# Gate values applied at the eviction of the expert rows instead of on the gathered rows

## The chip, the cores and the metric

One core of a Trainium2 chip runs one program. The metric is device time in microseconds (us) of one execution. The engines are named as in the profile: PE (matmuls; PEld is its weight load), ACT or ScalarE, DVE or VectorE, POOL or GpSimd (here mostly gathers, which are indirect DMAs), and SP, whose queue issues most DMAs.

## The reference, cut to what matters

The program is a block-sparse softmax attention (4 batches, 8 heads, 576 rows), then an expert layer with sticky routing, then a second, dense expert attention. The change is in the middle layer and at its seam with the last:

```python
logits = einsum('bsd,de->bse', x, w_gate)          # 8 experts
local_gate = sigmoid(x @ w_local)
for b: prev_e = -1
    for s:
        fresh_e = argmax(logits[b, s])
        e = fresh_e if s == 0 or local_gate[b, s] < 0.5 or prev_e < 0 else prev_e
        prev_e = e
        p = exp(logits[b, s] - max); p /= p.sum() + 1e-9
        h = maximum(x[b, s] @ w1[e], 0)             # 512 -> 1024
        out[b, s] = p[e] * (h @ w2[e])              # 1024 -> 512
x = out                                             # input of the last layer
```

`p[e]`, one number for each of the 2304 rows, is the gate value that the change moves.

## The kernel before

Stage 1 (`stage1`) computes attention for 16 pairs of heads. Its order is written out by hand: each step has a time in units of its own (W, EARLY, S0, TX0), and each engine runs its instructions in the order of these times, then in the order in which the later code emits them. S0 says when the copies of the first expert's weights (`split0`) are emitted: `split_high` makes a high part (f32r) on ScalarE and gives back a function that makes the low part on VectorE. At 146.70 stage 1 emits `rows_ev`, which copies the last rows out (`xraw`), and at 149.21 the copy `XT` on which the last logits rest.

`Route.main` then sorts the rows by expert. It is a chain of small steps, mostly on VectorE with small matmuls between (`small`). So that PE has work, `fill(i)` emits FILL[i] pieces of the first expert tile between them (`start`: 16 pieces of the first layer, six matmuls of 256 columns each, in four accumulators, and 16 of the second, three matmuls of 512 columns each). Their evictions (`hT_ev`) wait in `M.late` until they are popped or flushed. `inv` lists, for each slot of an expert tile, the row that it takes; `slot` lists for each row its slot. At the end of `main`, VectorE computes `psel`, the gate value of each row, in the layout of the rows (128 x 20), and `M.hoist` splits the last two of the first expert's w2 pieces (5 and 7).

`moe` runs the expert tiles of SEQ: pairs of 128 rows ("P") or tiles of 288 or 352 rows ("L"), t = 0 to 8. For each, the rows are fetched by POOL from `x_dram` through `inv` (`fetch`, four `xg` buffers, some two tiles ahead), turned (`tx`), put through the first layer (`g1`, accumulators `acc`) and the second (`g2`, banks `py`), and evicted by ScalarE (`y_ev`) to a tile that SP stores to `yg` in DRAM by slot. Before tile 1, LEFT says how many of the 32 pieces are left when each of its three transpositions is emitted; `M.tell` then writes the list of experts, from which SP reads the number of the expert for each weight load, and six `load()` of 1 MB each are emitted on SP. After the routing, a further pool `mop2` gives two more `acc` banks and one more `py` bank; `bank("py")` takes the two `py` banks of the first pool and then that one, in turn.

`stage3` fetches the rows of the expert layer from `yg` through `slot` (`fetch3`), and `xscale` multiplies them by `psel` (on VectorE for batch 0, on POOL for the others) before `txx` turns them.

Of the kernel before, what the change touches and what calls it, by code (L numbers as in the profile page):

```python
# [9 lines left out]
F32 = mybir.dt.float32  # L10
# [21 lines left out]
NCOL = 34  # L32
# [479 lines left out]
class Route:  # L512
# [224 lines left out]
    def main(self, fill, first):  # L737
# [47 lines left out]
        self.M.late.pop(0)()  # L785
        n = R[:, S - 1:S]
# [63 lines left out]
        first()  # L850
        slot = C.tile([128, 20], I32, name="slot")
# [41 lines left out]
        v.tensor_copy(erow[:, NT:], fl)  # L893
        den = W.tile([128, 20], F32, name="den")
        psel = C.tile([128, 20], F32, name="psel")
# [10 lines left out]
        self.slot, self.erow, self.psel = slot, erow, psel  # L906

        self.tell = lambda: v.tensor_copy(erow[:, 0:NT], er)
# [78 lines left out]
def moe_ops(nc, K, R, E, M, yg, W, bank, seq, reg):  # L987
# [108 lines left out]
    def y_ev(t, u, keep=False):  # L1096
        s = chunks(t)[u]
        c, m = cols(*seq[t])[u], s.stop - s.start
        y = R.row() if keep else E.tile([128, DM], F32, name="y", tag="xTP" + "hl"[ny[0] % 2])
        ny[0] += 1  # L1100
        if s.stop == width(t) and packed(t):
            lo = W.tile([128, DM], F32, name="ylo", tag="xg", bufs=4)
            nc.scalar.activation(lo[0:m], ys[t][u][m:2 * m], AF.Copy)
            nc.vector.tensor_tensor(y[0:m], ys[t][u][0:m], lo[0:m], op=ALU.add)
        else:
            nc.scalar.activation(y[0:m], ys[t][u][0:m], AF.Copy)
        if keep:
            late[c] = y[0:m]
        else:
            nc.sync.dma_start(yg[128 * c:128 * c + m], y[0:m])  # L1110
# [8 lines left out]
def moe(tc, nc, K, R, E, M, yg, W, ctx):  # L1119
# [24 lines left out]

    def gather():
        if rows:
            M.fetch(rows.pop(0))
# [27 lines left out]
    def start():  # L1175
        hT[0] = []
        for i in range(4):
            p = P1.tile([128, 512], F32, name="acc", bufs=2)
            for k in range(4):
                for f in range(2):  # L1180
                    h_mm(0, p[:, 256 * f:256 * f + 256], 2 * i + f, k, k == 0 and f == 0)
                if k == 3:
                    M.late.append(lambda p=p, i=i: hT_ev(0, p, i, 0))
                yield
        ys[0] = [bank("py") for _ in range(2)]
        for i in range(4):
            for u in range(2):
                for f in range(2):
                    y_mm(0, i, u, f)
                    if i == 3 and f == 1:  # L1190
                        M.late.append(lambda u=u: y_ev(0, u))
                    yield

    def hoist():
        for c in (5, 7):
            *wc[0, c], rest = split_high(nc, E, R.piece(0, c), 0, c)
            rest()
# [10 lines left out]
    P2.append(ctx.enter_context(tc.tile_pool(name="mop2", bufs=1, space=PSUM)))  # L1208
    M.last()
    ws, erow, fetch, fetch3, xscale = M.ws, M.erow, M.fetch, M.fetch3, M.xscale  # L1210
# [8 lines left out]
    for _ in range(6):  # L1219
        load()  # L1220
    for _ in pieces:
        M.flush()
# [35 lines left out]
    for j in range(4):  # L1258
        lab(xscale, 0, j)
# [6 lines left out]
def more(tc, nc, K, R, M, yg, ctx):  # L1266
# [12 lines left out]
    def again(kind, n, end):  # L1279
# [3 lines left out]
        with tc.If(nc.values_load(M.erow[0:1, f:f + 1], min_val=0, max_val=1) > 0):  # L1283
            seq.append((kind, n))
            t = len(seq) - 1
            for i, c in enumerate(cols(kind, n)):
                M.fetch(c, W)
                o.tx(t, i)
# [46 lines left out]
def stage3(tc, nc, K, ws, xr, fetch, xscale, row, out, last=None, nb=B):  # L1335
# [365 lines left out]
    for b in range(nb):  # L1701
        G = 2 * NJ * b
        for j in range(5):
# [38 lines left out]
FILL = (3, 1, 4, 2, 1, 1, 3, 2, 1, 1)  # L1742
# [5 lines left out]
S0 = ((138.5, 140), (140.3, 142), (144.7, 145.3), (144.95, 145.35), (146.68, None), (146.71, 146.9))  # L1748
LEFT = (13, 9, 4)
# [9 lines left out]
def model(tc, cst, qT, qx, kT, vp, tau, wgl, w12, wqk, wv, wo, out):  # L1759
    nc = tc.nc  # L1760
    with ExitStack() as ctx:
        C = ctx.enter_context(tc.tile_pool(name="c", bufs=1))
        DR = ctx.enter_context(tc.tile_pool(name="dr", bufs=1, space=DRAM))
        x_dram = DR.tile([B, S, DM], F32, name="x_dram")
        yg = DR.tile([NCOL * 128, DM], F32, name="yg")
        K = Consts(tc, nc, C, cst)
        L = C.tile([128, 5, B, 9], F32, name="L")
        with ExitStack() as mx, ExitStack() as rx:
# [3 lines left out]
            rt = Route(tc, nc, K, L, C, X, E)  # L1772
            M = Box()
            M.xg, M.split0, M.low, M.routed = {}, {}, {}, False
# [45 lines left out]
            M.late = []  # L1820
# [28 lines left out]
            def xscale(b, j):  # L1849
                x = xr[b, j]  # L1850
                eng = nc.gpsimd if b else nc.vector
                eng.tensor_scalar(x, x, rt.psel[:, 4 * j + b:4 * j + b + 1], 1.0, op0=ALU.mult, op1=ALU.mult)

            def last():
                rx.close()
                M.erow, M.tell = rt.erow, rt.tell
                M.ws = Weights3(tc, nc, ctx, wqk=wqk, wv=wv, wo=wo)

            M.fetch, M.fetch3, M.xscale, M.last = fetch, fetch3, xscale, last
            next(work)  # L1860
            rt.main(fill, first)
            M.routed = True
# [3 lines left out]
        done = stage3(tc, nc, K, ws, xr, fetch3, xscale, R.row, out)  # L1866

        f = 2 * (PMAX + LMAX)
        with tc.If(nc.values_load(M.erow[0:1, f:f + 1], min_val=0, max_val=1) > 0, preferred_fallthrough_block=True):
            with ExitStack() as rest, tc.manual_schedule():  # L1870
                more(tc, nc, K, R, M, yg, rest)
            for j in range(4):
                fetch3(0, j, j)
                xscale(0, j)
            stage3(tc, nc, K, ws, xr, fetch3, xscale, R.row, out, done)
# [64 lines left out]
```

## Time and profile before

| | us |
|---|---|
| median of 3 timed runs (744.45 to 745.25) | 745.1 |
| the profiled execution | 746.25 |
| its span, first to last instruction | 744.5 |
| PE busy | 721.5 (97%) |
| VectorE busy | 545.3 (73%) |
| ScalarE busy | 490.3 (66%) |
| POOL busy | 285.9 (38%) |

The page says how long each engine was busy, the chain of waits leads back from the last instruction, and the timeline shows each instruction with the idle time of its engine before it and, behind an arrow, what ended it. Stage 1 ends at about 285 us, routing and the first tile at about 316, the expert tiles at about 536. PE's clock was granted at full speed (0.998) throughout.

### The profile page before, as it was taken

To read this page: it belongs to the slowest core of one execution; us is meant where nothing else is said; L and a number is where in the kernel's file an instruction comes from. 1 tells how busy PE (TensorE), PEld (TensorE's weight loads), DVE (VectorE), ACT (ScalarE), POOL (GpSimd) and SP (SyncE) were. 2 spreads that over 40 slices of the span, in tenths; PEclk is the share of its full clock that TensorE was granted. 3 is DMA by queue.
4 is the path that set the end of the run, shared out by engine and by line. 5 is a ranking of instruction groups with operands and counts; after the bars stand their busy time and mean duration, and the time that the engine had idled before them with its cause. 6 is when DMAs were issued, how large, how long until landed. Compare 5 with 4: busy or idle time off the path is not lost.

```text
span 744.5 us, 14233 instructions
## 1 busy us (share of the span) xinstructions
PE 721.5 (97%) x5063; PEld 611.2 (82%) x5063; DVE 545.3 (73%) x1427; ACT 490.3 (66%) x1026; POOL 285.9 (38%) x442
## 2 busy tenths in 40 slices
PE   5999999999999999999999999999999999999996
PEld 4788887888887778798889889989788888888874
DVE  7998999899988988625575475554359888878780
ACT  5888888788887785334554455544256787777783
POOL 5888888887777892400110110000366000000000
PEclk9999999999999999999999999999999999999999
DMA  8448534444342431495855756601333000100103
GB/s 282 141 125 304 159 117 147 122 162 131 116 133 66 157 136 31 106 364 171 279 201 184 255 193 212 215 1 53 96 86 99 2 16 1 44 15 30 44 31 101
DMA packets 37408, 95.40 MB, mean 128 GB/s; under 512 B 4336, under 2 KB 14832, under 8 KB 33232
## 3 DMA queue, kind: packets, MB, share of 16 engines
q1 hardware_dynamic: 30960, 73.62, 29.1%
q0 software_dynamic: 5360, 19.34, 8.5%
q10 hardware_dynamic: 1008, 1.44, 0.6%
q8 instruction: 42, 0.69, 0.4%
q14 instruction: 38, 0.31, 0.1%
HBM read 75.58 MB, written 18.81 MB: 127 GB/s over the span
## 4 chain that ended last, share of the span: by engine, by line
PE 87%; DVE 7%; ACT 4%; issue 1%; DMA 1%; ACTq 0%; SPq 0%; DVEq 0%
PE py L1082 16%; PE acc L1053 15%; PE Y L336 11%; PE S L246 9%; PE X L293 8%; PE AV L1646 4%; PE X L1595 3%; PE Y L371 2%; PE S L251 2%; PE misc L1408 1%; PE misc L1409 1%; PE misc L1445 1%; PE S L1525 1%; PE misc L1410 1%; PE misc L1447 1%; PE misc L1446 1%
## 5 line engine op out<-in xcount | busy, mean ns | idle before, releaser
L280 DVE SCALAR_TENSOR_TENSOR P<-S,nm,E 128x576 f32<-128x576 f32 x144 | 116.4, 815 | 10.2 <-ACT E L267 4.6
L257 DVE TENSOR_REDUCE nm<-S 128x1 f32<-128x576 f32 x144 | 105.9, 754 | 17.6 <-PE S L246 16.8
L1082 PE MATMUL py<-w2h,hT 128*128 128x512 f32 (+2 forms) x344 | 114.8, 400 | 0.0
L267 ACT ACTIVATE E<-S,nm 128x576 f32<-128x576 f32 x144 | 104.1, 747 | 6.9 <-DVE nm L257 6.4
L246 PE MATMUL S<-KK,QS 128*128 128x288 f32 x256 | 84.2, 344 | 7.5 <-DVE QS L219 5.6
L293 PE MATMUL X<-cst,P 128*128 128x128 f32 x576 | 87.1, 278 | 1.4 <-ACT PT L304 0.7
L1777 POOL DMA_INDIRECT xg<-x_dram,inv x22 | 24.0, 1089 | 159.8 <-PE px L1011 128.2
L293 PEld LDWEIGHTS X<-cst,P 128*128 128x128 f32 x576 | 67.0, 142 | 16.1 <-issue 7.5
L304 ACT ACTIVATE PT<-X 128x512 f32<-128x512 f32 x128 | 75.7, 605 | 3.9 <-PE X L293 1.1
L1053 PE MATMUL acc<-xTh,w1h 128*128 128x256 f32 (+2 forms) x256 | 76.4, 299 | 0.0
L1053 PE MATMUL acc<-xTl,w1h 128*128 128x256 f32 (+2 forms) x256 | 76.0, 297 | 0.0
L1053 PE MATMUL acc<-xTh,w1l 128*128 128x256 f32 (+2 forms) x256 | 75.9, 297 | 0.0
L1082 PEld LDWEIGHTS py<-w2h,hT 128*128 128x128 f32 (+2 forms) x344 | 63.0, 183 | 15.4
L246 PE MATMUL S<-KL,QS 128*128 128x288 f32 x256 | 73.3, 300 | 0.3 <-DVE KL L201 0.3
L1082 PE MATMUL py<-w2l,hT 128*128 128x512 f32 (+2 forms) x176 | 69.5, 395 | 0.1
L336 PE MATMUL Y<-PT,v 128*64 128x320 f32 (+1 forms) x512 | 69.1, 412 | 0.2 <-ACT G L604 0.2
L1045 DVE SCALAR_TENSOR_TENSOR hT<-acc,hT 128x352 fp32r<-128x352 f32 (+3 forms) x60 | 30.4, 519 | 45.0 <-ACT hT L1042 45.0
L1042 ACT ACTIVATE hT<-acc 128x352 fp32r<-128x352 f32 (+2 forms) x52 | 26.2, 507 | 55.8 <-PE acc L1053 49.6
L246 PEld LDWEIGHTS S<-KK,QS 128*128 128x128 f32 x256 | 49.8, 194 | 9.0 <-issue 7.7
L336 PEld LDWEIGHTS Y<-PT,v 128*64 128x64 f32 x512 | 33.8, 136 | 24.5 <-issue 4.8
L1846 POOL DMA_INDIRECT raw<-yg,slot x18 | 17.6, 977 | 86.9 <-DMA yg<-y 62.0
L246 PEld LDWEIGHTS S<-KL,QS 128*128 128x128 f32 x256 | 50.0, 195 | 0.6 <-DVE KL L201 0.6
(397 smaller groups left out, 1920.6 us busy)
## 6 DMA issues: line engine op xcount, KB each, us to landing
raw<-in_w_dram SPq DMA_DIRECT2D x32, 1024.0 KB, 6.3
kraw<-in_kT_dram SPq DMA_DIRECT2D x15, 608.0 KB, 4.5
QS<-in_qT_dram POOLq DMA_DIRECT2D x15, 576.0 KB, 6.0
v<-in_vp_dram SPq DMA_DIRECT2D x16, 320.0 KB, 3.0
yg<-y SPq DMA_DIRECT2D x17, 256.0 KB, 5.0
qraw<-in_qx_dram SPq DMA_DIRECT2D x15, 288.0 KB, 2.7
x_dram<-xr SPq DMA_DIRECT2D x16, 256.0 KB, 2.5
yg<-raw SPq DMA_DIRECT2D x1, 3072.0 KB, 12.9
```

The lines of the kernel that those rows point to most:

```text
L246: nc.tensor.matmul(o, QS[p % NQ][:, a, cs], k[i][:, sl(576 * a)], start=(n == 0), stop=(n == 1))
L257: nc.vector.tensor_reduce(nm[:, 0:1], t[:, :, :288], axis=AX.XY, op=ALU.min)
L267: nc.scalar.activation(e, t[:, :, :288], AF.Exp, scale=-1.0, bias=nm[:, 0:1])
L280: nc.vector.scalar_tensor_tensor(PP[p, c][:, S * a:S * a + S].rearrange("p (h n) -> p h n", h=2), t[:, :, :288], nm[:, 1:2], e, op0=ALU.is ...
L293: nc.tensor.transpose(x[:, 128 * kc:128 * kc + 128], pp[:, o:o + 128], ident)
L304: nc.scalar.activation(PT[p, h][:, a, :, f:f + 128], x.rearrange("p (k q) -> p k q", k=4), AF.Copy)
L336: nc.tensor.matmul(out, l, r, start=s, stop=e, skip_group_check=True)
L1042: nc.scalar.activation(h[..., 0:w], p, AF.Relu)
L1045: nc.vector.scalar_tensor_tensor(h[..., low(t, c)], p[..., c], 0.0, h[..., c].bitcast(F32), op0=ALU.max, op1=ALU.subtract)
L1053: nc.tensor.matmul(o, a[:, fs], x[:, k, 0:w], start=(first and n == 0), stop=(k == 3 and n == 2), skip_group_check=True)
L1082: nc.tensor.matmul(ys[t][u][0:m], hT[t][i][:, f, k], w[:, 512 * f:512 * f + 512], start=(i == 0 and f == 0 and n == 0), stop=(i == 3 and f ...
L1646: nc.tensor.matmul(o[half(a), f:NH[h]], l, r, start=(k == 0), stop=(k == (1, 4)[h]), skip_group_check=True)
```

## The change

- `psel` is no longer computed at the end of `Route.main` but in a new function `scales`, called as `M.finish()` after `M.tell()` and the six `load()`. It now also turns `psel` on PE (a 128 x 20 transposition in the bank `prest`), copies the result on ScalarE (`pselT`) and stores it by row to DRAM with five DMAs on SP (4 partitions by up to 128 values each).
- `weigh(c)` is new: POOL gathers the gate values of the slots of column c from that DRAM tensor through `inv` into one column of `M.scale` (128 elements of 4 bytes). Nine columns (tiles 0 to 3) are gathered right after `M.finish()`, the 13 others each behind the fetch of its rows.
- `y_ev` multiplies by the column as it evicts (`scale=` of the activation; a second VectorE operation for the packed tail of tile 1). `xscale` is gone from stage 3.
- The evictions of tile 0 (`y_ev(0, u)`) no longer follow its last pieces but come after `g1(1, 2)`.
- The high parts of w2 pieces 5 and 7 are emitted earlier in `main` (after the scan `R`), their low parts after `first()` and where `hoist` stood. The copy of w2 piece 4 in stage 1 moves from 146.68 to 146.705, behind `rows_ev`.
- The first of the four accumulators of `start` takes a `py` bank. FILL and LEFT change; 22 pieces instead of 19 are emitted within `main`, and 27 instead of 28 before the third transposition. The pool `mop2` is opened after `M.finish()`.

```diff
@@ Route.main
         self.M.late.pop(0)()
+        self.M.hoist()
@@
         first()
+        self.M.lows[0]()
         slot = C.tile([128, 20], I32, name="slot")
@@
         nc.scalar.activation(ex, ex, AF.Exp)
-        self.M.hoist()
+        self.M.lows[1]()
         fill(8)
         self.flush()
+        self.slot, self.erow = slot, erow
+        self.tell = lambda: v.tensor_copy(erow[:, 0:NT], er)
+        self.finish = lambda: self.scales(ctx, W, ex, po, fl, pe, NT, px)
+
+    def scales(self, ctx, W, ex, po, fl, pe, NT, px):
+
+        nc, v = self.nc, self.nc.vector
         v.tensor_tensor(fl[:, NT:], fl[:, PMIN:PMIN + 1], fl[:, PMAX + LMIN:PMAX + LMIN + 1], op=ALU.max)
...
         v.tensor_tensor(psel, psel, den, op=ALU.mult)
-        for i in range(2):
-            v.tensor_copy(psel[64:128, 16 + 2 * i:17 + 2 * i], psel[0:64, 17 + 2 * i:18 + 2 * i])
+        pt = px[0:20, 128:256]
+        nc.tensor.transpose(pt, psel, self.K["ident"])
+        sT = W.tile([20, 128], F32, name="pselT")
+        nc.scalar.activation(sT, pt, AF.Copy)
+        for j in range(5):
+            w = min(128, S - 128 * j)
+            nc.sync.dma_start(self.psel[:, 128 * j:128 * j + w], sT[B * j:B * j + B, 0:w])
         ctx.close()
@@ y_ev
+        sc = M.scale[0:m, c:c + 1]
...
-            nc.vector.tensor_tensor(y[0:m], ys[t][u][0:m], lo[0:m], op=ALU.add)
+            nc.vector.tensor_tensor(lo[0:m], ys[t][u][0:m], lo[0:m], op=ALU.add)
+            nc.vector.tensor_scalar(y[0:m], lo[0:m], sc, None, op0=ALU.mult)
         else:
-            nc.scalar.activation(y[0:m], ys[t][u][0:m], AF.Copy)
+            nc.scalar.activation(y[0:m], ys[t][u][0:m], AF.Copy, scale=sc)
@@ moe
+    scaled = [c for t in range(4) for c in cols(*seq[t])]
+
     def gather():
         if rows:
-            M.fetch(rows.pop(0))
+            c = rows.pop(0)
+            M.fetch(c)
+            if c not in scaled:
+                M.weigh(c)
@@ start
-            p = P1.tile([128, 512], F32, name="acc", bufs=2)
+            p = P1.tile([128, 512], F32, name="acc", bufs=2) if i else PY.tile([128, 512], F32, name="py", bufs=2)
@@ moe
     M.tell()
     for _ in range(6):
         load()
+    M.finish()
+    for c in scaled:
+        M.weigh(c)
+    P2.append(ctx.enter_context(tc.tile_pool(name="mop2", bufs=1, space=PSUM)))
+    M.last()
     for _ in pieces:
         M.flush()
@@
             lab(g1, t, i)
             if t > 1:
                 splits(t, 4 + i)
+            elif i == 2:
+                for u in range(2):
+                    lab(y_ev, 0, u)
@@
-    for j in range(4):
-        lab(xscale, 0, j)
@@ stage3
                 at(G - 20 + j, 9, fetch, b, j)
-                at(G - 18 + j, 8, xscale, b, j)
@@
-FILL = (3, 1, 4, 2, 1, 1, 3, 2, 1, 1)
+FILL = (3, 1, 5, 2, 1, 1, 3, 2, 0, 4)
-S0 = ((138.5, 140), (140.3, 142), (144.7, 145.3), (144.95, 145.35), (146.68, None), (146.71, 146.9))
-LEFT = (13, 9, 4)
+S0 = ((138.5, 140), (140.3, 142), (144.7, 145.3), (144.95, 145.35), (146.705, None), (146.71, 146.9))
+LEFT = (10, 8, 5)
@@ model
+            def weigh(t):
+                nc.gpsimd.indirect_dma_start(out=M.scale[:, t:t + 1], out_offset=None, in_=rt.psel.rearrange("b (s o) -> (b s) o", o=1),
+                                             in_offset=bass.IndirectOffsetOnAxis(ap=rt.inv[:, t:t + 1], axis=0))
```

## Rows read from the trace of the kernel before

**Rows 1.** The page, busy time of each engine: us, share of span, instructions.

```profile
PE 721.5 (97%) x5063; PEld 611.2 (82%) x5063; DVE 545.3 (73%) x1427; ACT 490.3 (66%) x1026; POOL 285.9 (38%) x442
```

**Rows 2.** Table of stretches: busy us (and instructions) of each engine, clock, DMA.

```profile
540.00:560.00 20.00, 19.00 (x142) 17.52 (x141) 12.50 (x38) 11.52 (x31) 13.14 (x17) 1.00 0.30 82
```

**Rows 3.** Chain that ended last: start us, duration us, what; from 315 to 333.

```profile
315.82 12.73 PE acc L1053 x96
328.56 3.70 PE py L1082 x16
```

**Rows 4.** Timeline, PE in routing: start, duration, instruction, [idle before <- what ended it].

```profile
292.79 0.26 PE L765 MATMUL prest<-R,cst 32*32 32x1 f32 x4 [0.50 <-ACT hT L1042]
293.31 0.36 PE L1053 MATMUL acc<-xTPh,w1h 128*128 128x256 f32 x1 [0.27 <-DVE ti L795]
...
301.77 0.18 PE L765 MATMUL prest<-q,cst 32*1 32x23 f32 x1 [0.23 <-DVE q L859]
...
306.42 0.19 PEld L1082 LDWEIGHTS py<-w2l,hT 128*128 128x128 f32 x1 [0.57 <-DVE w2l L926]
```

**Rows 5.** Timeline, ACT at the end of stage 1.

```profile
282.58 1.06 ACT L925 ACTIVATE w2h<-raw 128x1024 fp32r<-128x1024 f32 x1
283.92 0.41 ACT L389 ACTIVATE xraw<-S 128x292 f32<-128x292 f32 x1 [0.28 <-DVE lg L387]
284.48 0.44 ACT L348 ACTIVATE XT<-Y 128x320 f32<-128x320 f32 x1
286.28 0.54 ACT L389 ACTIVATE xraw<-Y 128x438 f32<-128x438 f32 x1 [1.36 <-DVE lg L387]
```

**Rows 6.** Timeline, DVE: first and last step of the gate chain (11 instructions).

```profile
308.62 0.14 DVE L890 TENSOR_TENSOR fl<-fl 1x1 f32<-1x1 f32 x1
...
310.78 0.18 DVE L902 TENSOR_TENSOR psel<-psel,den 128x20 f32<-128x20 f32 x1
```

**Rows 7.** Timeline: third transposition of tile 1, `tell`, and SP's loads.

```profile
312.41 0.43 PE L1011 MATMUL px<-cst,xg 32*128 32x32 f32 x4
...
313.40 0.16 DVE L908 COPY erow<-er 1x23 int32<-1x23 int32 x1
...
314.54 4.62 SPq L979 DMA_DIRECT2D raw<-in_w_dram  x6
```

**Rows 8.** Line L979 on SP, issues from 314.5 and from 317.0: durations ns, landing us.

```profile
L979 SPq DMA_DIRECT2D raw<-in_w_dram x1: 368/368/368, 314.5 to 314.5; - x1
DMA to landing us min/median/max: 5.2/5.2/5.2
...
L979 SPq DMA_DIRECT2D raw<-in_w_dram x1: 333/333/333, 317.1 to 317.1; - x1
DMA to landing us min/median/max: 10.4/10.4/10.4
```

**Rows 9.** Lines L979 and L1110 on SP, a load and the store behind it.

```profile
L979 SPq DMA_DIRECT2D raw<-in_w_dram x1: 333/333/333, 366.0 to 366.0; - x1
DMA to landing us min/median/max: 5.7/5.7/5.7
...
L1110 SPq DMA_DIRECT2D yg<-y x1: 332/332/332, 366.9 to 366.9; - x1
DMA to landing us min/median/max: 5.4/5.4/5.4
```

**Rows 10.** The page, DMA issues of `x_dram`: count, KB each, median us to landing.

```profile
x_dram<-xr SPq DMA_DIRECT2D x16, 256.0 KB, 2.5
```

**Rows 11.** Line L1846 on POOL, the 18 gathers from `yg`: us to landing.

```profile
DMA to landing us min/median/max: 3.4/3.5/3.6
```

**Rows 12.** Timeline, ACT: the first eviction of expert rows.

```profile
314.46 0.60 ACT L1106 ACTIVATE y<-py 128x512 f32<-128x512 f32 x1 [1.30 <-PE py L1082]
```

**Rows 13.** Timeline, start of stage 3: DVE's fifth multiplication, PE's wait.

```profile
543.56 0.49 DVE L1852 TENSOR_SCALAR raw<-raw,psel 128x512 f32<-128x512 f32 x1 [0.62 <-DMA raw<-yg,slot]
...
545.91 0.35 PE L1526 MATMUL S<-k3l,q3s 128*128 128x256 f32 x1 [0.17 <-DVE k3l L1429]
```

More of the change, by code (lines that the diff above doesn't have):

```diff
@@ L892, in main @@
         v.tensor_scalar(fl[:, NT:], fl[:, NT:], 1.0, None, op0=ALU.min)
-        v.tensor_copy(erow[:, NT:], fl)
+        v.tensor_copy(self.erow[:, NT:], fl)
         den = W.tile([128, 20], F32, name="den")
-        psel = C.tile([128, 20], F32, name="psel")
+        psel = W.tile([128, 20], F32, name="psel")
         v.tensor_reduce(den, ex, axis=AX.X, op=ALU.add)
@@ L1189, in start @@
                     y_mm(0, i, u, f)
-                    if i == 3 and f == 1:
-                        M.late.append(lambda u=u: y_ev(0, u))
                     yield
@@ L1196, in hoist @@
             *wc[0, c], rest = split_high(nc, E, R.piece(0, c), 0, c)
-            rest()
+            M.lows.append(rest)
     M.bank, M.hoist = bank, hoist
@@ L1206, in moe @@
         yield
-    P2.append(ctx.enter_context(tc.tile_pool(name="mop2", bufs=1, space=PSUM)))
-    M.last()
-    ws, erow, fetch, fetch3, xscale = M.ws, M.erow, M.fetch, M.fetch3, M.xscale
+    fetch, fetch3 = M.fetch, M.fetch3
     for i in range(3):
@@ L1220, in moe @@
         load()
+    M.finish()
[3 more added lines that the diff above has]
+    M.last()
+    ws = M.ws
     for _ in pieces:
@@ L1287, in again @@
                 M.fetch(c, W)
+                M.weigh(c)
                 o.tx(t, i)
@@ L1332, in store, with stage3 @@
             eng.dma_start(out[b - 1 + a, 512:576], o[64 * a:64 * a + 64])
-def stage3(tc, nc, K, ws, xr, fetch, xscale, row, out, last=None, nb=B):
+def stage3(tc, nc, K, ws, xr, fetch, row, out, last=None, nb=B):
     ctx = ExitStack()
@@ L1764, in model @@
         x_dram = DR.tile([B, S, DM], F32, name="x_dram")
+        psel = DR.tile([B, S], F32, name="psel")
         yg = DR.tile([NCOL * 128, DM], F32, name="yg")
@@ L1772, in model @@
             rt = Route(tc, nc, K, L, C, X, E)
+            rt.psel = psel
             M = Box()
+            M.scale = C.tile([128, NCOL], F32, name="scale")
             M.xg, M.split0, M.low, M.routed = {}, {}, {}, False
@@ L1818, in model @@
             work = moe(tc, nc, K, R, E, M, yg, W, mx)
-            M.late = []
+            M.late, M.lows = [], []
             def flush():
@@ L1847, in fetch3 @@
                                              in_offset=bass.IndirectOffsetOnAxis(ap=rt.slot[:, 4 * j + b:4 * j + b + 1], axis=0))
[L1849 to L1852, printed above, removed]
+            def weigh(t):
+                nc.gpsimd.indirect_dma_start(out=M.scale[:, t:t + 1], out_offset=None, in_=rt.psel.rearrange("b (s o) -> (b s) o", o=1),
+                                             in_offset=bass.IndirectOffsetOnAxis(ap=rt.inv[:, t:t + 1], axis=0))
             def last():
                 rx.close()
-                M.erow, M.tell = rt.erow, rt.tell
                 M.ws = Weights3(tc, nc, ctx, wqk=wqk, wv=wv, wo=wo)
-            M.fetch, M.fetch3, M.xscale, M.last = fetch, fetch3, xscale, last
+            M.fetch, M.fetch3, M.weigh, M.last = fetch, fetch3, weigh, last
             next(work)
             rt.main(fill, first)
-            M.routed = True
+            M.routed, M.erow, M.tell, M.finish = True, rt.erow, rt.tell, rt.finish
             for _ in work:
@@ L1865, in model @@
             ws = M.ws
-        done = stage3(tc, nc, K, ws, xr, fetch3, xscale, R.row, out)
+        done = stage3(tc, nc, K, ws, xr, fetch3, R.row, out)
         f = 2 * (PMAX + LMAX)
@@ L1873, in model @@
                 fetch3(0, j, j)
-                xscale(0, j)
-            stage3(tc, nc, K, ws, xr, fetch3, xscale, R.row, out, done)
+            stage3(tc, nc, K, ws, xr, fetch3, R.row, out, done)
 _INS = ["cst", "qT", "qx", "kT", "vp", "tau", "wgl", "w12", "wqk", "wv", "wo"]
```

2 lines of the change are left out of this document (removed).

## The prediction

> **What bounds the kernel now.** I read the page's busy line first: PE is busy 721.5 us of 744.5 [rows 1], so time moves only where PE is made to wait or an existing wait goes. The table of stretches says where PE still waits in the second half: 1.0 us in 540 to 560 [rows 2], where stage 3 starts. The chain of waits through the first expert tiles consists of PE work: the 96 first-layer matmuls of the second tile (t = 1) from 315.82 for 12.73 us, then its second layer at 3.70/16 = 0.231 us a matmul [rows 3]. In time order I then read PE's waits in routing [rows 4], ScalarE ahead of it [rows 5], VectorE's gate chain [rows 6], and the queue of SP [rows 7] with its landings [rows 8, 9]. A "piece" below is one step of the first tile's work that `fill` hands out: three matmuls of 0.231 (or six of half that), 0.70 us.
>
> The profiled execution took 746.25 us: a span of 744.5 and 1.75 around it. The median of the three timed runs is 745.1, that is 1.15 below the profiled one. I sum on the trace's own times and carry the difference to 745.1. About 0.2% (1.5 us) is what a measurement can tell from no change.
>
> **The change part by part.**
>
> *Front of routing.* One more piece (FILL[2] from 4 to 5) runs before the counts, and covers PE's wait of 0.50 at 292.79; putting the first accumulator in a `py` bank removes the 0.27 at 293.31, where the accumulator of the next piece is waited for [rows 4]. Against that, S0 moves the copy of w2h piece 4 (1.06 us at 282.58) behind `xraw`, which waits for VectorE and starts at 283.92 [rows 5]. The copy filled that hole; now it starts at 284.33 and holds the `XT` copy from 284.48 to about 285.4. `XT` feeds the last logits, so routing moves by +0.9. The extra piece gives back 0.70 and the bank the rest: net -0.1. Bounds: -0.9 if `XT` isn't delayed, and +0.1.
>
> *Index list to `tell`.* The copies of w2 pieces 5 and 7 run early on ScalarE, their low parts on VectorE under four pieces. That removes the weight wait of 0.57 at 306.42 and the 0.23 at 301.77 [rows 4]; with smaller ones I take 1.05. One piece fewer stands ahead of the third transposition (27, not 28): -0.70. So it moves from 312.41 [rows 7] by -0.1 - 1.05 - 0.70 to 310.55, and the end of `tell` from 313.56 to 311.7.
>
> *The gate chain and its turn.* Behind `tell` VectorE does what stood from 308.62 to 310.96, 2.34 us [rows 6], and only then can PE turn `psel`. The turn is issued ahead of the last five pieces, so PE waits from 310.95 (end of the transposition) to 311.7 + 2.34 = 314.05: 3.1 us, then 0.2 for the turn (a quarter of a transposition of 0.43 [rows 7] and the change over) and 5 x 0.70. The second tile begins at 317.75 where it began 2.1 us before. This is a new wait, with nothing ahead of it on PE to fill it. Without it the tile would begin 1.0 early.
>
> *The stores, and the wait that decides.* `finish` stands behind six `load()` on SP. In the trace the first load is issued 0.98 after `tell` ends, and six take 4.62 us to issue [rows 7]. The first lands 5.2 after its issue at 314.5, the fourth 10.4 after 317.1, that is 13.0 after the first issue [rows 8]: one after the other, 2.6 apart. The sixth would land 16.5 to 18.4 after the first issue; I take 17.6. A store issued behind a load waits for it: the load of 366.0 lands at 371.7, and the store issued at 366.9 lands at 372.3, 5.4 after its issue [rows 9], where a store with little ahead takes 2.5 [rows 10]. So I take the five stores of `psel` as landed 0.9 after the last load (bounds 0 and 2). First issue 311.7 + 1.0 = 312.7; sixth landing 330.3; `psel` 331.2. POOL's gather of the first scale column then takes 3.5 to landing [rows 11] (the nearest row; of 4-byte elements there is none, bounds 2.5 and 5): 334.7. `y_ev(0, 0)`, 0.60 us on ScalarE [rows 12], ends at 335.35.
>
> The Trainium skill (DMA: Bandwidth & Descriptors, Queues, rings and completion order) has a rule that weakens this step: completion isn't in order per issuing queue, and a later transfer on one engine may signal while an earlier one on sixteen still runs. By the rows the sum is the one below; if the rule lets the four rows of `psel` through, it is the first rival.
>
> Who waits: `y_ev(0, 0)` is issued behind the evictions of `g1(1, 2)`, at about 327.5, and ScalarE stands for 7 us with the last evictions of tile 1 and the next transposed rows behind it. PE goes through `g1(1, 3)`, whose banks are free, to 330.5, and through the first chunk of `g2` (six matmuls, 1.4 us, in the bank of `mop2`) to 331.9. The second chunk needs the `py` bank that `y_ev(0, 0)` frees. It began at 328.56 + 1.4 = 329.95; now at 335.4: +5.5. The +2.1 above is inside this, since this wait would absorb it. The third chunk's bank follows one gather later, under six matmuls. POOL's other columns are used tiles later, and the fetches behind them are two tiles ahead. The second multiply of the packed tail (about 0.49 us of VectorE, as in [rows 13]) lies beside PE's first layer of tile 2.
>
> *Stage 3.* The multiplications by `psel` go from VectorE and POOL. Four of VectorE's five lie under PE's matmuls. The fifth waits 0.62 for its gather at 543.56 and then runs 0.49, with the low part of k behind it; PE waits for that part at 545.91 [rows 13]. I take -0.6 of the 1.0 us that PE stands in this stretch [rows 2]; bounds 0 and -1.5. POOL's multiplications lie beside everything. Its 13 later gathers of one column stand between fetches that are two tiles ahead: nothing.
>
> Sum: +5.5 - 0.6 = +4.9: a span of 749.4, or 750.0 us against the median. By the bounds (landing 16.5 to 18.4, `psel` 0 to 2, gather 2.5 to 5, stage 3, the front; not all at one end) between about 747.8 and 752.5.
>
> **The rivals.**
>
> *The rows pass the loads (746.6 us).* If these stores come through within 2.5 to 4 us of issue, `psel` is there by about 322 and the first column by 326, before ScalarE comes to `y_ev` at 327.5. Then only the wait at the turn is left: +2.1 - 0.6 = +1.5; it is 745.7 if `XT` isn't delayed. For it: four rows of 512 B are little against loads of 1 MB. Against it: [rows 9]. This is what the Trainium skill's rule above (DMA: Bandwidth & Descriptors, the same section) would give; no row shows a four-row store behind loads.
>
> *Faster: the turn has cover (743.3 us).* If the five pieces are issued ahead of the turn (3.5 us, more than the 3.1 of the wait), PE doesn't stand there; if the column is also there by the time of `y_ev`, what stays is -1.0 at the start of tile 1 and -0.6 in stage 3, and a little more if `XT` isn't delayed: -1.6 to -2.4. It decides at the turn: VectorE would have to end the chain by 311, or PE have 3 us of pieces ahead of it. Against it: in [rows 4, 6, 7] the engines keep the order of the code.
>
> *Slower still (752.4 us).* The first accumulator's `py` bank may be one that the end of stage 1 still holds; the last rows are read out of theirs until 286.82 [rows 5], up to 2.4 us behind PE's first piece, which shifts routing and `tell` by as much: 750.0 + 2.4. Gathers of single elements that land after more than 5 us would do the same.
>
> *It doesn't do what it says:* no sign of that; the multiply is an operand of an activation that runs anyway.
>
> **How the numbers follow.** The forecast 0.62 (747.8 to 752.5), the passing rows 0.17 (some two thirds of it within 0.2%, the rest above), the covered turn 0.13, the slower bank 0.08. The time is that of the first, 750.0. The range 745.5 to 752.6 leaves out the covered turn and part of the slower case, about 0.2. Faster by over 0.2% (below 743.6): 0.13; within: 0.11; slower (above 746.6): 0.76.
>
> **What would show it.** Right: PE idle some 3 us ahead of the turn, released by VectorE's `psel`; the six loads landing one by one and the `psel` rows behind the last; ScalarE idle for some 7 us before `y_ev(0, 0)`, released by a gather; PE waiting about 3.5 us before its second chunk of `g2(1, 0)`, released by `y_ev`; 0.6 us less in 540 to 560. Wrong: `psel` rows landing in the middle of the loads; no idle PE at the turn; `XT` at 284.5 as before; or a stage 3 shorter by more than 1.5 us, which would mean that the multiplications there held more than the one wait.

## The result, and the profile after

| | before | after |
|---|---|---|
| median of the timed runs, us | 745.17 (4 runs, 744.45 to 745.69) | 754.39 (4 runs, 753.48 to 755.08) |
| after / before, 95% interval | | 1.0123 [1.0111, 1.0135] |
| the profiled execution | 746.25 | 753.48 |
| its span | 744.5 | 751.7 |
| mean granted clock of PE | 0.998 | 0.990 |

The change makes the kernel slower by 9.2 us (1.2%); the forecast was 4.9, with 752.6 as its upper end. The two profiled executions differ by 7.2: the one of before lies 1.1 above its median, the one of after 0.9 below. So the two traces can explain 7.2; the other 2.0 lie in the spread between executions, which these traces don't divide.

The busy line of the page, after; PE has 2 us more [rows 1], the rest of the 7.2 is waiting:

```profile
PE 723.5 (96%) x5064; PEld 614.0 (82%) x5064; DVE 539.3 (72%) x1421; ACT 491.5 (65%) x1027; POOL 302.4 (40%) x451
```

Then PE's waits, first from 283 to 345 us (routing, first tiles), then from 537 to 620 (start of stage 3): who waited for what, us in total, times, longest.

```profile
PE prest L913 <- DVE psel L911: 2.9, 1, 2.9
PE py L1093 <- ACT y L1119: 1.5, 1, 1.5
```

```profile
PE misc L1430 <- DVE x3l L1414: 3.9, 1, 3.9
```

The waits of [rows 4] are gone. Two stand for them, at the turn of `psel` and at the bank that `y_ev(0, 0)` frees; both were forecast. The third, 3.9 us in stage 3, was not. Before, the longest in that stretch was:

```profile
PE misc L1408 <- DVE q3s L1423: 1.1, 1, 1.1
```

To divide the 7.2 us I use a marker that both traces have: the first PE transpositions of stage 3's batches (the tile `misc` from `raw`, twelve at a time). Before, then after:

```profile
536.46 1.47 PE L1380 MATMUL misc<-cst,raw 128*128 128x128 f32 x12
...
556.67 1.74 PE L1380 MATMUL misc<-cst,raw 128*128 128x128 f32 x12
```

```profile
541.33 1.47 PE L1402 MATMUL misc<-cst,raw 128*128 128x128 f32 x12
...
560.66 1.69 PE L1402 MATMUL misc<-cst,raw 128*128 128x128 f32 x12
```

| stretch | before | after | difference |
|---|---|---|---|
| to the first marker (routing, expert tiles) | 536.5 | 541.3 | +4.9 |
| between the markers | 20.2 | 19.3 | -0.9 |
| from the second marker to the end of the span | 187.8 | 191.0 | +3.2 |

The first two lines are the forecast nearly as it stood; the error is in the third. Here is what stands there. ACT and PE, then POOL of after (start, duration, instruction, idle before and what ended it):

```profile
568.08 0.38 ACT L1444 ACTIVATE q3s<-misc 64x256 fp32r<-64x256 f32 x1 [5.09 <-PE S L1548]
569.52 0.60 ACT L1413 ACTIVATE x3h<-misc 128x512 fp32r<-128x512 f32 x1 [1.06 <-remote]
...
564.43 0.28 PE L1432 MATMUL misc<-x3h,wqkl 128*128 128x256 f32 x1
...
570.89 0.64 PE L1430 MATMUL misc<-x3h,wqkh 128*128 128x320 f32 x1 [3.93 <-DVE x3l L1414]
```

```profile
559.50 0.97 POOL L1870 DMA_INDIRECT raw<-yg,slot  x1 [0.15 <-POOL k3l L1389]
...
567.02 0.95 POOL L1870 DMA_INDIRECT raw<-yg,slot  x1 [0.30 <-issue]
569.75 0.94 POOL L1870 DMA_INDIRECT raw<-yg,slot  x1 [1.79 <-remote]
```

ScalarE stands for 5.09 us before `q3s`, though the matmuls that it evicts were over by about 564.7: some 3.4 us in which nothing that it needs is open. Then "remote" and "issue" stand as releasers, also for POOL itself: names for "nothing that the trace can show". All this happens while POOL sends eight gathers, seven of them 1.25 us apart without a pause. Before, `xscale` stood between them; at most three followed one another (565.69, 567.02, 568.27):

```profile
561.17 0.94 POOL L1846 DMA_INDIRECT raw<-yg,slot  x1 [0.30 <-issue]
562.14 0.71 POOL L1852 TENSOR_SCALAR raw<-raw,psel 128x512 f32<-128x512 f32 x1
563.31 0.70 POOL L1852 TENSOR_SCALAR raw<-raw,psel 128x512 f32<-128x512 f32 x1 [0.46 <-DMA raw<-yg,slot]
```

Two more things stand in the trace of after. The loading of instructions isn't what the engines wait for: from 554 to 579 us there is no such transfer. And the nine scale columns, in a row from 331.39, do the same where it costs nothing: transposed rows that PE had ready by 341.7 are evicted at 345.74, after 4.84 us of idle ScalarE behind "remote", while PE has other work.

The clock has a part too. Table of stretches of after (busy us of PE, PEld, DVE, ACT, POOL, then the granted clock, DMA share, GB/s): behind the wait at the turn, and behind the stall of stage 3.

```profile
313.60:316.70 3.10, 2.87 (x8) 2.29 (x9) 0.17 (x1) 0.27 (x1) 0.00 (x0) 0.50 1.00 330
...
570.90:576.00 5.10, 5.10 (x21) 5.10 (x22) 4.29 (x24) 2.89 (x9) 0.00 (x0) 0.50 0.18 51
```

Both times PE had stood (2.87 and 3.93 us) and got 0.50 afterwards, 1.2 instead of 2.4 GHz. The wait costs more than its length. The forecast had nothing for it.

### The profile page after: what moved, and what is told of

Same layout as the page of the kernel before. It is cut to its first block, busy times and chain, and to the rows that moved or that the text cites. A ratio compares the mean times of both kernels' runs of the same rounds, so it can differ in the third digit from the quotient of the medians.

```text
span 751.7 us, 14259 instructions
## 1 busy us (share of the span) xinstructions
PE 723.5 (96%) x5064; PEld 614.0 (82%) x5064; DVE 539.3 (72%) x1421; ACT 491.5 (65%) x1027; POOL 302.4 (40%) x451
## 4 chain that ended last, share of the span: by engine, by line
PE 88%; ACT 4%; DMA 3%; DVE 3%; issue 1%; ACTq 0%; SPq 0%; DVEq 0%; POOLq 0%
PE py L1093 16%; PE acc L1064 13%; PE Y L336 11%; PE S L246 9%; PE X L293 8%; PE AV L1668 4%; PE X L1617 3%; PE Y L371 3%; PE misc L1430 2%; PE misc L1431 2%; PE misc L1432 2%; PE S L251 2%; PE S L1548 1%; DMA raw<-in_w_dram 1%; PE S L1547 1%
```

## The experiments

The theory after the first reading: (A) up to stage 3 the loss is the late scale column, and the wait at the turn lies inside it; (B) in stage 3 it is POOL's gathers in a row, which `xscale` used to hold apart. The rivals: the wait at the turn costs by itself; the stall is an accident of one execution; the loss comes from POOL or VectorE having other work beside PE. Medians are in us, with the ratio to the kernel before, timed together with each.

### The turn and the stores

*The same kernel once more*: does the stall of stage 3 belong to the program?

> The changed kernel once more, to see whether the stall that its profile shows at 563 to 571 us in stage 3 (ScalarE idle for 5.09 us before a copy whose input matmuls ended some 3 us earlier; PE idle for 3.9 us, then at a granted clock of 0.5 to 576) belongs to the program. If it does: the same stall within 1 us of the same place, span about 751 to 753 us. If it is chance in one execution: no stall there, span about 748.5 us (751.7 less 3.2).

752.02, span 750.2. The stall is there again, cut differently (ACT's timeline, then PE's waits from 540 to 620):

```profile
567.76 0.60 ACT L1413 ACTIVATE x3h<-misc 128x512 fp32r<-128x512 f32 x1 [2.46 <-PE S L1548]
...
570.68 0.38 ACT L1449 ACTIVATE k3k<-misc 64x256 fp32r<-64x256 f32 x1 [1.36 <-remote]
```

```profile
PE misc L1430 <- issue: 2.5, 1, 2.5
```

It is the program's. From the second marker (560.36) to the end it takes 189.8, 2.0 more than before where the first execution had 3.2: the price varies between executions.

*The stores of `psel` on ScalarE's queue* instead of SP's, so not behind the loads:

```
-            nc.sync.dma_start(self.psel[:, 128 * j:128 * j + w], ...
+            nc.scalar.dma_start(self.psel[:, 128 * j:128 * j + w], ...
```

> The five stores of the turned gate values are issued on ScalarE's queue; nothing else is changed. Theory (they wait on SP's queue behind six loads of 1 MB): the values land some 3 us after the turn, by 319 us instead of 330.6; the first eviction of expert rows no longer waits for its scale column; what stays is the wait at the turn with the slower clock behind it, 3.1 us at the first evictions of tile 1, instead of 4.8: 754.4 - 1.7 = 752.7 us. Rival (the loads' traffic on the shared DMA engines delays the rows whatever the queue): landing still after 325, and 754 us.

752.77, 1.0104 [1.0088, 1.0121]. The number came, but not on the way that was expected. POOL and ScalarE of this kernel, then PE's wait behind the turn:

```profile
322.47 0.94 POOL L1874 DMA_INDIRECT scale<-psel,inv  x1 [11.92 <-DMA psel<-pselT]
...
328.13 0.41 ACT L1053 ACTIVATE hT<-acc 128x288 fp32r<-128x288 f32 x1 [2.12 <-PE acc L1064]
334.55 0.41 ACT L1053 ACTIVATE hT<-acc 128x288 fp32r<-128x288 f32 x1 [6.00 <-remote]
```

```profile
PE py L1093 <- issue: 2.0, 1, 2.0
```

The first gather starts at 322.47 instead of 331.39, so the queue was what held the rows (A). But now nine gathers and a fetch in a row fall into tile 1, and ScalarE stands again for 6.00 us behind "remote": the picture of stage 3 in another place. PE meets 2.0 us of it. The gain of one wait was spent on another.

*The turn with cover*: the last five pieces ahead of it, so that PE needn't wait for `psel`.

```
+    for _ in pieces:
+        M.flush()
+    M.flush()
     M.finish()
...
-    for _ in pieces:
-        M.flush()
-    M.flush()
```

> The last five pieces of the first tile are issued ahead of the gate chain and its turn, which stay as they are otherwise. Theory (the wait of the first eviction for its column decides, and absorbs the wait at the turn): PE's 2.9 us at the turn and the granted clock of 0.5 behind it are gone, the second tile begins by 315, PE waits 4 to 5 us at the first eviction instead of 1.5, and the time is unchanged: 754.4 us, within 0.8. Rival (the turn decides): the second tile and all behind it come 3 us earlier, 751.4 us.

755.22, 1.0143 [1.0126, 1.0160]: no gain over the change. The wait at the turn is gone, and one wait of 5.9 stands for both. PE's waits from 300 to 345, then the stretch around that wait:

```profile
PE py L1093 <- ACT y L1119: 5.9, 1, 5.9
```

```profile
330.00:336.00 6.00, 1.69 (x4) 1.41 (x5) 0.15 (x1) 1.86 (x4) 3.77 (x4) 0.53 0.11 37
```

The half clock moved with it: 0.53 from 330 to 336, and 1.00 around the turn. So up to stage 3 one thing decides, the late column, as (A) says.

### Stage 3

*The multiplications back in stage 3, by 1.0* (the gate values still come in at the eviction):

```
...
+            def space(b, j):
+                x = xr[b, j]
+                eng = nc.gpsimd if b else nc.vector
+                eng.tensor_scalar(x, x, 1.0, 1.0, op0=ALU.mult, op1=ALU.mult)
```

> In stage 3 the gathered rows are multiplied by 1.0 where the kernel before multiplied them by the gate values (VectorE for batch 0, POOL for the others); all else is as in the changed kernel. Theory (without the multiplications POOL issues eight gathers back to back, and these cause the stall at 563 to 571 us): POOL's gathers are spaced as before, no stall, a granted clock of 1.0 throughout stage 3: 754.4 - 3.2 + 0.8 = 752.0 us. Rival (the stall has to do with something else, as where the program's instructions lie): it stays, and the 0.8 us that the multiplications cost are added: 755.2 us.

751.02, 1.0094 [1.0075, 1.0113], 2 to 3 us less than the change by its distance to before (2.2 by the ratios, 3.0 by the medians). POOL and PE's waits of this kernel in stage 3:

```profile
566.34 0.64 POOL L1879 TENSOR_SCALAR raw<-raw 128x512 f32<-128x512 f32 x1
567.68 0.62 POOL L1879 TENSOR_SCALAR raw<-raw 128x512 f32<-128x512 f32 x1 [0.70 <-DMA raw<-yg,slot]
```

```profile
PE misc L1432 <- DVE q3s L1447: 1.1, 1, 1.1
```

The stall is gone; PE's longest wait is 1.1, as in before. Work that changes no number makes the kernel faster: (B) by adding.

*Before, without POOL's 13 multiplications* (nothing else of the change): (B) by taking away.

```
-                at(G - 18 + j, 8, xscale, b, j)
+                if not b:
+                    at(G - 18 + j, 8, xscale, b, j)
```

> The kernel before with only POOL's 13 multiplications of stage 3 left out (batches 1 to 3 go on without their gate values); nothing of routing or of the expert tiles is touched. Theory (gathers that POOL issues back to back hold the other engines up): eight gathers stand 1.25 us apart from about 555 us on, ScalarE waits 2 to 5 us for matmuls that have ended, PE stands 2.5 to 4 us: 744.8 + 2.5 to 4 = 747.3 to 748.8. Rival (the forecast's: these multiplications lie beside everything): 744.8, within 0.5.

747.95, 1.0044 [1.0028, 1.0061]: leaving work out costs 3.3 us. The stall of after stands in the kernel before (ACT, POOL, PE's waits):

```profile
563.58 0.38 ACT L1422 ACTIVATE q3s<-misc 64x256 fp32r<-64x256 f32 x1 [6.03 <-remote]
...
563.87 0.94 POOL L1847 DMA_INDIRECT raw<-yg,slot  x1 [1.87 <-remote]
```

```profile
PE misc L1408 <- DVE x3l L1392: 3.7, 1, 3.7
```

Neither the gate columns, nor the stores, nor the turn is there: what stage 3 lost needs nothing else of the change.

*Before, without VectorE's five multiplications*: what the forecast's -0.6 rested on.

```
-    for j in range(4):
-        lab(xscale, 0, j)
...
-                at(G - 18 + j, 8, xscale, b, j)
+                if b:
+                    at(G - 18 + j, 8, xscale, b, j)
```

> The kernel before with only VectorE's five multiplications of stage 3 left out (batch 0 goes on without its gate values). Theory (the forecast's stage 3): the wait of the fifth goes with what PE stood for it, -0.6: 744.2 us, the start of the third stage's scores 0.6 to 0.8 earlier. Rival (they lie wholly under PE's matmuls): 744.8.

744.51, 0.9997 [0.9987, 1.0007]: nothing that can be measured, though the interval (-1.0 to +0.5 us) doesn't exclude -0.6. In the trace the two markers stand 19.6 us apart (535.93 to 555.56) against 20.2.

*Before, with POOL's multiplications cut to 16 of 512 columns*: is it their length that holds the gathers apart, or that they wait for the landing?

```
+                x = x[:, 0:16] if b else x
```

> The kernel before with POOL's 13 multiplications of stage 3 cut from 512 columns to 16 (the other 496 go on without their gate values). POOL still waits for each gather's landing, but computes next to nothing. Theory (what keeps the stall of e5_before_nopool away is that POOL waits for landings, so that few gathers stand at once): no stall, 744.6 us within 0.7. Rival (it is the time that POOL computes, 0.7 us each): the stall is there, 747 to 748 us.

743.66, 0.9983 [0.9974, 0.9993]: no stall, with 0.3 us of work for each instead of 0.7. POOL:

```profile
562.89 0.28 POOL L1853 TENSOR_SCALAR raw<-raw,psel 128x16 f32<-128x16 f32 x1 [1.25 <-DMA raw<-yg,slot]
```

It is the pause for the landing that counts, not the work behind it. A pause of the same length with no landing to wait for was not run.

### A row of gathers by itself

*Before, with nine extra gathers* of 128 x 1 from `x_dram` through `inv`, whose values nobody uses, right behind the loads:

```
+    for t in range(9):
+        M.extra(t)
```

> The kernel before with nine extra gathers of 128 x 1 elements on POOL behind the six loads (their values are used nowhere); no gate value, store or eviction is moved. Theory (a row of gathers on POOL holds the other engines up by itself): they run 1.25 us apart from 314.4 to 325.6; ScalarE waits 2 to 6 us, to about their end, for matmuls of tile 1 that ended earlier; PE, with four accumulators, stands 0 to 3 us: 744.6 to 747.6. Rival (it took the change's own waits, on the scale columns, to hold ScalarE up): no wait of ScalarE beyond the 1.2 us of its usual rhythm, 744.6.

745.34, 1.0001 [0.9992, 1.0010]. The row runs from 310.08 to 321.3. One of ScalarE's evictions of tile 1, which are 1.5 to 1.7 us apart as in before, and the nine landings:

```profile
320.25 0.41 ACT L1042 ACTIVATE hT<-acc 128x288 fp32r<-128x288 f32 x1 [1.24 <-PE acc L1053]
```

```profile
DMA to landing us min/median/max: 2.5/7.4/8.2
```

This is a miss for the plain form of (B), "a row of gathers holds others up".

*The same nine behind the fetch of tile 3.* They ran from 313.66 to 324.6, not from 334 as the expectation has it, since that fetch stands at 312.41: 3.6 us later than in the run above, and no more.

```
+                if (t, i) == (1, 0):
+                    for c in range(9):
+                        M.extra(c)
```

> The kernel before with nine extra gathers of 128 x 1 elements on POOL (their values are used nowhere) behind the fetch that follows tile 2's first transposition: from about 334 to 345 us, in the place where they stood in the changed kernel, when the six loads have landed. Theory (a row of gathers holds others up, but in e9_nine_extra it was over before it counted): ScalarE's transposed rows of tile 2 (336.87 in the kernel before) come 0.8 to 4 us late against PE's transposition; the time moves by 0 to 2. Rival (extra gathers alone hold nothing up): no event of PE is seen late by more than 0.1 us, 744.6.

752.19, 1.0104 [1.0089, 1.0120]: 7.5 us for nine gathers that nobody waits for. ACT and PE in the timeline, then PE's waits:

```profile
316.82 0.41 ACT L1042 ACTIVATE hT<-acc 128x288 fp32r<-128x288 f32 x1 [1.05 <-PE acc L1053]
326.66 1.01 ACT L1042 ACTIVATE hT<-acc 128x288 fp32r<-128x288 f32 x3 [9.43 <-remote]
...
323.09 0.29 PE L1053 MATMUL acc<-xTh,w1l 128*128 128x288 f32 x1 [1.32 <-issue]
```

```profile
PE acc L1053 <- issue: 3.7, 4, 1.7
```

PE stands in the middle of an accumulation group, where it needs nothing of anyone, and ScalarE misses three evictions, the first due at about 318.4, 4.7 us after the row began. So a row can hold other engines up by itself, and need not.

*The same nine, POOL waiting for each*: a multiplication by 1.0 on each column.

```
+                c = M.scale[:, t:t + 1]
+                nc.gpsimd.tensor_scalar(c, c, 1.0, 1.0, op0=ALU.mult, op1=ALU.mult)
```

> As e13_nine_late (nine extra gathers of 128 x 1 in the kernel before, their values used nowhere), but behind each of them POOL multiplies its column by 1.0, and so waits for its landing before the next. Theory (several gathers that stand at once hold the other engines up, one at a time does not): ScalarE's evictions of tile 1 come 1.6 us apart again, no wait of PE in 316 to 330: 744.7 us within 0.8, against 752.2 with the nine unchecked. Rival (that there are nine more gathers in this place is enough): 749 to 752 us.

745.48, 1.0005 [0.9996, 1.0015]: 752.2 goes back to 745.5. POOL and ACT:

```profile
319.36 0.19 POOL L1857 TENSOR_SCALAR scale<-scale 128x1 f32<-128x1 f32 x1 [4.85 <-DMA scale<-x_dram,inv]
319.70 0.99 POOL L1854 DMA_INDIRECT scale<-x_dram,inv  x1
...
319.92 0.41 ACT L1042 ACTIVATE hT<-acc 128x288 fp32r<-128x288 f32 x1 [1.24 <-PE acc L1053]
```

The same nine gathers, never two of them under way at once, cost nothing. What separates the first run from the second is open. In the first, three landed 2.5 to 3.6 us after their issue, before the weight loads came, and the six others after 6.7 to 8.2; in the second all run beside the loads. A limit on the gathers under way doesn't explain it by itself: by these landings six were under way at 320.1 in the first run, and nothing was late; in the second only four of the nine had been sent when the first eviction fell due. Nor does the data pile up in stage 3 of after: between 560.9 and 570.3 the queue moved the 1.8 MB of seven gathers, as fast as POOL sent them. Nothing was run at a set count.

### What the change can give without its waits

*Stores on ScalarE's queue, five columns gathered at once, the others behind later fetches.*

```
-    for c in scaled:
+    for c in scaled[:5]:
...
+        if M.begun and behind:
+            M.weigh(behind.pop(0))
```

> Stores on ScalarE's queue as in e2_actq; of the nine scale columns only the first five are gathered at once, the other four one by one behind the next fetches. In e2_actq ScalarE waited 6.0 us, to 334.55, for a matmul result of 329, while nine gathers and a fetch stood back to back from 322.5 to 334.6. Theory (the row of gathers holds ScalarE up): with five it waits at most 1 us, PE's 2.0 us before 335.6 and the granted clock of 0.5 behind it go: 752.8 - 2.0 - 1.7 = 749.1 us. Rival (ScalarE waited for the scale column, or for its stores): as e2_actq, 752.8.

751.46, 1.0092 [1.0075, 1.0108]: 1.1 less than the nine by the distance to before, where 3.7 less was expected. PE's 2.0 us at `y_ev` are gone; the stall of stage 3 is still there, and seven gathers in a row (321.77 to 330.2, a fetch among them) still hold evictions of tile 1 up, one by 3.45 us at 328.93.

*All of it*: the run above with the turn covered and POOL's multiplications by 1.0 in stage 3.

> Four of the edits at once: the five pieces ahead of the turn, the stores on ScalarE's queue, five scale columns at once and the others behind fetches, and POOL's multiplications of stage 3 kept, by 1.0. Theory (turn, stores behind loads and rows of gathers are all that the change lost): the second tile begins 1 us earlier than in the kernel before, no new wait follows, stage 3 gains 0.6: 744.8 - 1.6 = 743.2 us. Rival (another wait takes their place, as the first eviction of expert rows behind a scale column that comes after 328): 745 to 748 us.

744.85, 0.9996 [0.9986, 1.0006]: some 9 us better than the change, level with before, 1.7 short of what was expected. PE still stands 0.9 at `y_ev`, where ScalarE waits for the column until 328.76.

*Two columns at once, the others two by two* (`scaled[:2]`):

> As e8_combined, but only the two scale columns of the first tile are gathered at once; the seven others go two by two behind the next fetches. Theory (in e8_combined the five gathers from 322.7 still delay the first eviction to 328.76 and PE by 0.9): the first eviction by 327, no wait of PE, 744.85 - 0.9 = 743.9 us. Rival (the column comes late because of its stores and the loads): as e8_combined, 744.85.

744.48, 0.9993 [0.9984, 1.0002]: the 0.9 stays. So it isn't the number of gathers in a row; what is left is the way of the values to DRAM and back, beside the loads, which the version with the early stores below bears out.

*With the copy of w2 piece 4 back at its place of before* (S0 146.68):

> As e10_combined_two, with the copy of w2 piece 4 back at its old place in stage 1 (S0 at 146.68), ahead of the copy that gives the last logits. Theory (the forecast's front: the move delays the last logits, and routing, by 0.7 to 0.9): routing 0.7 earlier, 743.9 - 0.7 = 743.2 us. Rival (the copy delays rows or logits by itself at its old place): within 0.3 of e10_combined_two.

744.09, 0.9987 [0.9977, 0.9996]: 0.4 less than the run above, within what can be measured. `XT` starts at 284.77 instead of 285.16 in the change.

*With the gate chain back at the end of `main`, the turn right behind the third transposition, the stores ahead of the loads* (still on ScalarE's queue; all else as in the run above):

```
-        self.finish = lambda: self.scales(ctx, W, ex, po, fl, pe, NT, px)
+        self.finish = self.turn
+        self.scales(ctx, W, ex, po, fl, pe, NT, px)
...
+    M.finish()
     M.tell()
     for _ in range(6):
         load()
-    M.finish()
```

> As e11_combined_s0, but VectorE runs the gate chain at the end of the routing, where it stood before the change, and PE turns its result right behind the third transposition; the stores go out on ScalarE's queue ahead of the six loads. Theory (in e11_combined_s0 the column of the first eviction comes late, at about 328.5, since stores and gather share the DMA engines with the loads): the values land by 316, the column by 321, no wait of PE at the first eviction: 744.1 - 1.0 = 743.1 us. Rival (the chain ahead of the list of experts holds the loads back, and tile 2 waits for its weights): 744 to 746 us.

743.18 (11 runs), 0.9981 [0.9972, 0.9990]: the best of all, 1.5 us below before. POOL, ACT and PE's only wait from 283 to 345:

```profile
317.50 0.94 POOL L1894 DMA_INDIRECT scale<-psel,inv  x1 [8.56 <-DMA psel<-pselT]
...
325.04 1.26 ACT L1126 ACTIVATE y<-py,scale 128x512 f32<-128x512 f32 x2
```

```profile
PE px L1029 <- DVE xTl L1035: 0.7, 1, 0.7
```

The column is there before ScalarE comes to it. What of the 1.5 us comes from the front, where the waits of [rows 4] are gone, and what from VectorE's five multiplications was not separated. POOL's work in stage 3 is all still there.

*The change, with POOL waiting for each column and 16 columns of work in stage 3*: does the wait alone mend it?

> The changed kernel, with such a multiplication by 1.0 on POOL behind each gather of a scale column (one column) and behind each gather of stage 3's batches 1 to 3 (16 columns); turn, stores and evictions stay as they are. Theory: the stall of stage 3 goes as in e4_space, the columns cost nothing more, and what is left is the turn and the stores behind loads: 751.0 us (as e4_space), down to 750. Rival (waiting for each landing makes the columns late for the evictions of tile 1): 752 us and more.

755.72, 1.0152 [1.0134, 1.0170]. The stall of stage 3 is gone (PE's longest wait there is 1.2), but the columns now come one per 3 to 6 us, and the fetches queued behind them on POOL come late (POOL, then PE's waits from 300 to 400):

```profile
366.26 0.98 POOL L1803 DMA_INDIRECT xg<-x_dram,inv  x1
```

```profile
PE px L1022 <- DMA xg<-x_dram,inv: 2.7, 1, 2.7
PE py L1093 <- ACT y L1119: 2.3, 2, 1.6
```

The next follows at 367.55; in the change the two were issued at 343.6 and 344.8. A pause on POOL is only free where nothing urgent is queued behind it.

*The best version with the same short waits*:

> e14_early, with the multiplications of stage 3 cut to 16 columns as in e12_small and one behind each scale column. Theory: ScalarE's evictions at 323.2 and 324.7, some 1.4 us late in e14_early behind five gathers, come on time, and stage 3 gains what e12_small gained (1.0): 743.2 - 1.0 = 742.2 us. Rival (neither is on the path here): 743.2.

743.95, 0.9986 [0.9977, 0.9995]: no gain over 743.18; a wait of 1.1 at `y_ev` is back.

## Why the forecast was right in direction and too small

*Front of routing.* Right. `XT` starts at 285.16, 0.7 later (forecast +0.9), behind the copy of w2 piece 4 at 284.20; the waits of [rows 4] are gone.

*Index list to `tell`.* Right: third transposition at 310.52 (forecast 310.55), end of `tell` at 311.66 (311.7).

```profile
310.52 0.43 PE L1022 MATMUL px<-cst,xg 32*128 32x32 f32 x4
313.83 0.38 PE L913 MATMUL prest<-cst,psel 128*20 128x128 f32 x1 [2.87 <-DVE psel L911]
...
311.51 0.15 DVE L893 COPY erow<-er 1x23 int32<-1x23 int32 x1
```

*The turn.* The wait was sized right (2.87, forecast 3.1). Not forecast was the clock of 0.50 behind it: tile 1's first eviction comes at 320.60, some 3.1 later than before where the forecast had 2.1. It cost nothing more, since the next wait took it in, as the forecast says of the 2.1; the covered turn ended no earlier.

*The stores and the deciding wait.* Right, a little too large. SP, POOL and ACT of after:

```profile
312.68 3.99 SPq L990 DMA_DIRECT2D raw<-in_w_dram  x6
316.77 7.27 SPq L918 DMA_DIRECT2D psel<-pselT  x5
...
331.39 0.94 POOL L1874 DMA_INDIRECT scale<-psel,inv  x1 [20.92 <-DMA psel<-pselT]
...
333.79 0.69 ACT L1119 ACTIVATE y<-py,scale 128x512 f32<-128x512 f32 x1 [4.88 <-DMA scale<-psel,inv]
...
334.53 0.50 PE L1093 MATMUL py<-w2h,hT 128*128 128x512 f32 x1 [1.49 <-ACT y L1119]
```

First load 312.68 (forecast 312.7); `psel` releases POOL at 331.39 (331.2 for its landing); column to `y_ev` 2.4 instead of 3.5, which is the term that was too large; PE resumes at 334.53 (335.4): +4.6 against +5.5. ScalarE stood 4.9 us, not 7, and PE 1.5, not 3.5, because both came to the place later, behind the half clock (ScalarE by 1.4, PE by 1.1), and the column was there 0.9 sooner. The Trainium skill's rule (DMA: Bandwidth & Descriptors, Queues, rings and completion order), that completion isn't in order per queue, did not help these rows: their packets moved at 329.0 to 329.3, when 6.2 MB of the six loads' 6.3 had moved. With the stores on the other queue POOL got them at 322.47, in the middle of the loads; that agrees with what the same section says of the DMA engines taking turns between queues.

*Stage 3: the step that failed.* "POOL's multiplications lie beside everything. Its 13 later gathers of one column stand between fetches that are two tiles ahead: nothing." VectorE's part holds in the trace (-0.9 between the markers, forecast -0.6, bounds 0 and -1.5), though leaving out the five alone can't be told from nothing in the median. POOL's part has the wrong sign: its multiplications weren't only work, they made POOL wait for each landing and so kept the gathers apart. Without them the stretch behind the second marker is 3.2 us longer, and before loses 3.3 by the same cut. Term by term, the stretches measured +4.9 (forecast +5.5), -0.9 (-0.6) and +3.2 (nothing), together +7.2, the difference of the spans. (The forecast's total, also +4.9, equals the first of them by chance.)

I had asked of POOL's multiplications only what waits for them, not what they themselves wait for. [Rows 13] shows the same form on VectorE: a multiplication that stands until its gather has landed.

*The rivals.* The passing rows fall (331.39); the covered turn falls (2.87 of wait); of the slower bank there is no sign, as PE has no wait between 283 and the turn. "Slower still" (752.4) came nearest in its number, but the mechanism was one that none of the rivals named, and the range ended 1.8 below the result because it held no term of that kind. Where the rest of the 9.2, beyond 7.2, is lost isn't shown; five executions of the changed kernel lie between 752.02 and 755.08.

## What to carry to other kernels

Before an operation that "lies beside everything" is taken away, ask what it waits for and what stands behind it on its queue: a wait may be what keeps transfers apart. A value that goes through DRAM is best stored ahead of the large loads, or on another queue, and its consumer placed behind the time of the whole round trip; the multiplication that it saves may not be worth that. When a wait is forecast on PE, a price for the clock behind it belongs into the range.

## What the runs showed of the hardware

- Gathers that POOL sends in a row can hold up engines that have nothing to do with them: 7.5 us for nine of 128 x 1 elements, 3.3 us for eight fetches of stage 3. In four places the first event that came late was due 4.7 to 5.2 us after the first gather of the row (nine extra ones 4.7, stores on ScalarE's queue 4.7, five columns 4.9, stage 3 of after 5.2); elsewhere it was 4.3 (the best version), 5.7 (before without POOL's multiplications) and 6.2 (the change's nine columns), so no fixed number of gathers comes out of it. With POOL waiting for each landing the cost went to 0.5 or less. In one run nine cost nothing. Even the best version has a trace of it: with five in a row from 317.50 (a fetch among them) the eviction due at 321.8 comes at 323.23, and costs nothing there. What is held up inside the chip is not shown.
- PE's granted clock was 0.50 (1.2 GHz) once it had stood for 2.87 and 3.93 us, over the next 3.1 and 5.1 us of work; around a stand of 5.9 us it was 0.53 over 6 us. In before, with no wait above 1.1 us in these stretches, it was 1.00.
- Five stores of a few 512-byte rows took from their first issue until POOL was released 14.6 us behind six loads on the same queue (316.77 to 331.39), 8.0 on ScalarE's queue among the loads (314.51 to 322.47), and still 6.8 on that queue when issued ahead of the loads (310.68 to 317.50), where a store with little beside it takes 2.5 [rows 10].
